# Turning w3 on VectorE in squares of 32 instead of on TensorE

## The chip, the cores and the metric

The kernel runs on one core of a Trainium2 chip. The metric is the device time of one execution in microseconds (us). The core has a matrix engine (TensorE, PE in the profile; its weight loads are shown apart as PEld), VectorE (DVE), ScalarE (ACT), GpSimd (POOL) and SyncE (SP), which here issues the DMAs. Each engine works through its own instructions in order; a semaphore joins them where one needs the result of another. TensorE writes to PSUM, which has eight banks; the other data lie in SBUF, 128 partitions wide.

## What is computed

An mLSTM cell runs over 4 batches, 8 heads, 768 time steps and head size 40. Its output, 3072 tokens of 320 numbers, goes through a multiplicative feed-forward network. The inputs are float64 in memory.

```python
for t in range(S):
    m_new = np.maximum(f_gate[:, :, t] + m, i_gate[:, :, t])
    ...
    C = f_stab[:, :, None, None] * C + i_stab[:, :, None, None] * np.einsum('bhd,bhe->bhde', vt, kt)
    ...
    y[:, :, t] = o * h_tilde / denom
# x: (3072, 320); w1, w2: (320, 1024); w3: (1024, 1024); w_out: (1024, 320)
a = x @ w1
b = x @ w2
h = a * b @ w3
return h @ w_out
```

## The kernel before

**Folding.** The kernel doesn't compute `a * b @ w3` for every token. It folds the two last matrices into one, `w3o = w3 @ w_out` (1024 x 320), and then computes `(a * b) @ w3o`. For the fold, TensorE needs `w3` with its columns on the partitions: for each of eight blocks `ko` of 128 rows of `w3`, a turned tile `w3T[ko]` of 128 partitions by 8 x 128. `w3_mm(ko)` (L240) multiplies its eight squares `w3T[:, ki, :]` with the eight blocks `wo[:, ki, :]` of `w_out`, sums them in the PSUM tile `wp`, and ScalarE brings the sum to `w3o[:, ko, :]`.

**Weights.** They come from memory as pairs of 32-bit words, into one of four `raw` buffers (two parts of the tile `w3o` help out at the start). `fetch` (L179) issues the load of the next of 34 tiles, at most three tiles ahead of the conversions: ten of `w1`/`w2`, eight of `w_out` (128 x 320), sixteen halves of `w3` blocks (128 rows by 512 columns). ScalarE scales the high words (`scale`, L154, the row `raw<-raw`). Then `to_f32` (L158) makes float32 of them with five VectorE instructions (L167 to L171: `ex`, `ex`, `ma`, `ma`, and the target). The fourth one, L170, is the last reader of a `raw` buffer; after it the buffer is free for another load.

**Turning.** A `w3` half that has been converted is put on the list `later`. In the next step `fold` (L216) turns it: `w3_trans` (L228) lets TensorE transpose four squares of 128 x 128 into a PSUM tile `w3p`, and the tile is copied to `w3T`, the first half of a block by VectorE (L238), the second by ScalarE (L236). One step later `fold` runs `w3_mm` of that block.

**Steps.** The main loop has 30 steps `s`; the first 24 run one quarter of work of the cell each (one batch, 128 time steps), the later ones only the network. A step gives TensorE, in this order: `turn(s)`, eight transposes of `k` and `q` (`pt`); `x_trans`, three transposes of the cell's output of two steps before (`px`); `fold` (`wp`, `w3p`); from step 17 on the products with `w3o` (`po`); the products with `w1` and `w2` of two groups (`pa`, `pb`, L499), which step 9 and the steps after it do with 256 columns at a time; their remainders with `wr`; and the cell (`quarter_work`, L292). TensorE's order is fixed by the program. The other engines follow the written order up to step 6 (`pinned`); behind it a scheduler orders them by the readiness that it foresees.

**What waits for what.** `pa` and `pb` are brought together by ScalarE (`a_sb<-pa`, L519) and VectorE (`ab<-pb,a_sb`, L520). All of `pt`, `px`, `wp`, `w3p`, `pa` and `pb` take their turn in four PSUM banks, so the `pt` and `px` of a step use the banks of the `pa` and `pb` of the step before: TensorE waits there until `a_sb` and `ab` of that step are done. In the cell, VectorE multiplies the scores with the weights (`pw<-cell,pw`, L330), which the cell of the next step needs; behind it come the state, `h`, `den` and `y` (L334 to L367), and `y` is turned two steps later.

**SP's queue.** A step's DMAs are issued in the order: two loads `pw<-U_d`, then `k`, `q`, `v`, `o_in`, for two or three steps ahead, then the `raw` loads of that step. SP waits in order for whatever a load's buffer must be free of. Eight semaphores go round for SP's DMAs, so each DMA also waits for the landing of the eighth one before it.

**Which tile when.** By the list `n_cvt`, step 4 and step 5 convert two tiles, steps 6, 7 and 8 three, steps 9 to 15 two. The `w_out` tiles are converted in the steps up to 8, the first `w3` block in step 8, and so on to the last in step 15. So the `w3p` of the first block stand in step 9, its `wp` in step 10, and the last `wp` in step 17.

Of the kernel before, what the change touches and what calls it, by code (L numbers as in the profile page):

```python
# [8 lines left out]
FP = mybir.dt.float32  # L9
# [7 lines left out]
def kernel(  # L17
# [26 lines left out]
    nc = tc.nc  # L44
# [12 lines left out]
    DFF = moe_w1.shape[1]  # L57
    FO = DFF // P
# [7 lines left out]
    wst = ctx.enter_context(tc.tile_pool(name="wst", bufs=2))  # L66
# [15 lines left out]
    def in_order(ins):  # L82

        if last:
            tc.add_manual_dep(ins.ins, last.pop().name, mybir.DependencyInfo(
                mybir.DependencyClass.NoSync, mybir.DependencyReason.DATA), reason="in_order")
        last.append(ins.ins)

    def mm(out, lhsT, rhs, start=True, stop=True):
        in_order(nc.tensor.matmul(out, lhsT=lhsT, rhs=rhs, start=start, stop=stop))  # L90

    def transpose(out, in_, n=P):
        in_order(nc.tensor.transpose(out, in_, ident[0:n, 0:n]))  # L93
# [44 lines left out]
    wo = const.tile([128, FO, DM], FP, name="wo")  # L138
# [4 lines left out]
    CW = 512  # L143
    w1_d, w2_d, w3_d, wo_d = (x.bitcast(U32) for x in (moe_w1, moe_w2, moe_w3, moe_w_out))
# [3 lines left out]
    def raw_tile(n, pieces):  # L148
        raw = idle.pop(0) if idle else wst.tile([128, n, 2], U32, name="raw", tag="raw", bufs=4)
        for r, src in pieces:  # L150
            nc.sync.dma_start(out=raw[r].rearrange("p n two -> p (n two)"), in_=src)
        return raw

    def scale(raw):  # L154
# [3 lines left out]
    def to_f32(dst, raw):  # L158

        n = dst.shape[-1]
        lo, hi = raw[:, :, 0], raw[:, :, 1]
        t = wst.tile([128, n], U32, name="ex", tag="ex", bufs=1)
        r = wst.tile([128, n], U32, name="ma", tag="ma", bufs=1)
        V = nc.vector
        V.tensor_scalar(out=t, in0=hi, scalar1=3, scalar2=None, op0=OP.logical_shift_left)  # L167
        V.scalar_tensor_tensor(out=t, in0=hi, scalar=0x80000000, in1=t, op0=OP.bitwise_and, op1=OP.bitwise_or)  # L168
        V.tensor_scalar(out=r, in0=t, scalar1=0xFF800000, scalar2=None, op0=OP.bitwise_and)
        V.scalar_tensor_tensor(out=r.bitcast(FP), in0=lo, scalar=2.0 ** -52, in1=r.bitcast(FP), op0=OP.mult, op1=OP.mult)  # L170
        V.tensor_tensor(out=dst, in0=t.bitcast(FP), in1=r.bitcast(FP), op=OP.add)  # L171

    def cols(c0, n):
        return slice(2 * c0, 2 * (c0 + n))

    every = slice(0, 128)
    pend, scaled = [], []

    def fetch(kind, i, part):  # L179

        if kind == "w12":
            c0 = part * CW
            if i < 2 * KF:
                wt, src = ((w1, w1_d), (w2, w2_d))[i // KF]
                ko = i % KF
                dst, pieces = wt[:, ko, c0:c0 + CW], [(every, src[ko * 128:(ko + 1) * 128, cols(c0, CW)])]
            else:
                dst, pieces = wr[:, c0:c0 + CW], [(slice(j * REM, (j + 1) * REM), src[KF * P:DM, cols(c0, CW)])
                                                  for j, src in enumerate((w1_d, w2_d))]
        elif kind == "wo":  # L190
            dst, pieces = wo[:, i, :], [(every, wo_d[i * 128:(i + 1) * 128, :])]
        else:
            c0 = part * CW
            dst, pieces = None, [(every, w3_d[i * 128:(i + 1) * 128, cols(c0, CW)])]
        pend.append((dst, raw_tile(dst.shape[-1] if dst is not None else CW, pieces), i, part))

    later = []

    def scale_next():
        scaled.append(pend.pop(0))  # L200
        scale(scaled[-1][1])

    def convert():
        if not scaled:
            scale_next()
        dst, raw, ko, half = scaled.pop(0)
        if dst is None:
            dst = wst.tile([128, CW], FP, name="w3", tag="w3")
            to_f32(dst, raw)
            later.append((dst, ko, half))  # L210
        else:
            to_f32(dst, raw)

    turned_w3 = []

    def fold():  # L216
        while turned_w3:
            w3_mm(turned_w3.pop(0))
        while later:
            w3, ko, half = later.pop(0)  # L220
            w3_trans(w3, ko, half)
            if half:
                turned_w3.append(ko)


    w3T_t = {}

    def w3_trans(w3, ko, half):  # L228
        if half == 0:
            w3T_t[ko] = wst.tile([128, FO, 128], FP, name="w3T", tag="w3T")  # L230
        tp = mps([128, FO // 2, 128], "w3p")
        for j in range(FO // 2):
            transpose(tp[:, j, :], w3[:, j * 128:(j + 1) * 128])
        r = slice(half * (FO // 2), (half + 1) * (FO // 2))
        if half:
            nc.scalar.copy(out=w3T_t[ko][:, r, :], in_=tp)  # L236
        else:
            nc.vector.tensor_copy(out=w3T_t[ko][:, r, :], in_=tp)  # L238

    def w3_mm(ko):  # L240
        w3T = w3T_t.pop(ko)
        wp = mps([128, DM], "wp")
        for ki in range(FO):
            mm(wp, w3T[:, ki, :], wo[:, ki, :], start=(ki == 0), stop=(ki == FO - 1))
        nc.scalar.mul(out=w3o[:, ko, :], in_=wp, mul=UP ** -2)
# [293 lines left out]
    todo = w12[KF * 2 + 1:] + [("wo", i, 0) for i in range(FO)] + [("w3", ko, part) for ko in range(FO) for part in range(2)]  # L539
# [5 lines left out]
    for s in range(len(n_up)):  # L545
# [48 lines left out]
        for _ in range(n_cvt[s] if s < len(n_cvt) else 0):  # L594
            convert()
            converted += 1
# [4 lines left out]
            for ins in keep_order(front):  # L601
                behind.enter_context(tc.issue_after(ins))
    behind.close()
    assert not ups and not downs and not todo and not pend and not later and not turned_w3, (len(ups), len(downs), len(todo), len(pend))
# [1 line left out]
_INS = ['q', 'k', 'v', 'i_gate', 'f_gate', 'o_gate', 'moe_w1', 'moe_w2', 'moe_w3', 'moe_w_out']  # L606
_OUTS = [((3072, 320), 'float32')]
# [25 lines left out]
```

## Time and profile before

| | |
|---|---|
| median of 3 runs | 510.38 us (509.05 to 511.63) |
| the profiled execution | 509.16 us |
| its span on the core | 507.1 us |
| busy: PE, PEld, DVE, ACT, POOL | 472.5, 387.7, 242.7, 161.1, 87.0 us |
| mean granted clock of TensorE | 0.975 |

The span is what the trace covers; some 2 us of the time lie around it. The page's slices cut the span into 40 equal parts, with the busy share of each engine in tenths, and PEclk as the clock that TensorE was granted, in tenths of full speed. A chain of waits goes from the last instruction back to whatever released each one. A row of the timeline reads: start and duration in us, engine, line, operation, out<-in by the program's names, shape, count, and in brackets how long the engine sat idle before it and what ended that. Windows give the busy time of each engine in a stretch. Engine names with a q (SPq) are the queues that issue DMAs.

### The profile page before, as it was taken

The page shows a single profiled execution, that of the slowest core. Times are in us where ns is not written, and L with a number is a line of the kernel's source. Part 1 is how long each engine was busy: PE and PEld are TensorE (multiplying, and loading weights), DVE is VectorE, ACT ScalarE, POOL GpSimd, SP SyncE. Part 2 cuts the span into 40 slices and gives each one's busy share as a digit, 9 for nine tenths or more (in the row PEclk, how much of TensorE's full clock was granted, in tenths as well). Part 3 has the DMA queues.
Part 4 walks back from the last instruction along what each step waited for, and adds up shares of the span by engine and source line. Part 5 has one row for each costly group of instructions (what it writes and reads, how often), then busy time and mean ns, then how long its engine had stood idle before and what let it go on. Part 6 is the DMA issues. An engine that isn't in the chain of part 4 may idle for free.

```text
span 507.1 us, 13454 instructions
## 1 busy us (share of the span) xinstructions
PE 472.5 (93%) x5778; PEld 387.7 (76%) x5778; DVE 242.7 (48%) x504; ACT 161.1 (32%) x421; POOL 87.0 (17%) x163
## 2 busy tenths in 40 slices
PE   3869788896999999999999999999999999899997
PEld 2759677795888788888877777877778778677874
DVE  7787698999877568665440404224032141210110
ACT  4734446355334433523341414222122011111011
POOL 5532223433112111211220202111000000000000
PEclk9979998996999999999999999999999999999999
DMA  8999856599743535421331314131000000000001
GB/s 184 167 207 188 168 104 135 123 220 227 192 115 75 145 107 106 74 49 28 74 63 38 63 38 89 40 74 27 27 14 15 27 13 15 27 0 27 1 14 39
DMA packets 112203, 42.32 MB, mean 83 GB/s; under 512 B 101968, under 2 KB 105232, under 8 KB 112144
## 3 DMA queue, kind: packets, MB, share of 16 engines
q1 hardware_dynamic: 112000, 41.37, 38.5%
q8 instruction: 45, 0.74, 0.7%
q14 instruction: 14, 0.11, 0.1%
q10 hardware_dynamic: 144, 0.10, 0.1%
HBM read 37.42 MB, written 4.03 MB: 82 GB/s over the span
## 4 chain that ended last, share of the span: by engine, by line
PE 77%; DVE 9%; issue 7%; POOL 2%; DMA 2%; ACT 1%; SPq 0%; DVEq 0%; POOLq 0%; ACTq 0%
PE pa L90 21%; PE po L90 20%; PE pb L90 14%; PE cell L90 8%; PE wp L90 7%; PE pt L93 3%; DMA raw<-in_moe_w_dram 2%; DVE h L355 2%; PE w3p L93 1%; PE px L93 1%; PE ub L90 1%; DVE ex L168 1%; DVE ma L170 1%; DVE o_in L365 1%; POOL pw L270 1%
## 5 line engine op out<-in xcount | busy, mean ns | idle before, releaser
L520 DVE TENSOR_TENSOR ab<-pb,a_sb 128x512 f32<-128x512 f32 x48 | 33.2, 691 | 195.6 <-ACT a_sb L519 191.2
L90 PE MATMUL po<-w3o,ab 128*128 128x320 f32 x384 | 105.4, 433 | 1.3 <-DVE h L355 1.3
L90 PEld LDWEIGHTS po<-w3o,ab 128*128 128x128 f32 x384 | 72.2, 190 | 30.7 <-issue 1.5
L90 PE MATMUL pa<-xT,w 128*128 128x256 f32 (+1 forms) x448 | 94.3, 358 | 0.1
L90 PE MATMUL pb<-xT,w 128*128 128x256 f32 (+1 forms) x448 | 92.1, 351 | 0.3 <-issue 0.3
L90 PEld LDWEIGHTS pa<-xT,w 128*128 128x128 f32 x448 | 77.1, 196 | 10.5 <-ACT a_sb L519 0.8
L90 PEld LDWEIGHTS pb<-xT,w 128*128 128x128 f32 x448 | 76.4, 192 | 9.1 <-issue 0.5
L519 ACT ACTIVATE a_sb<-pa 128x512 f32<-128x512 f32 x48 | 28.5, 593 | 117.8 <-PE pb L90 117.8
L289 POOL TENSOR_TENSOR state<-state,decay 128x164 f32<-128x164 f32 x40 | 19.7, 496 | 186.5 <-PE cell L90 132.2
L90 PE MATMUL pb<-xT,wr 64*64 64x256 f32 (+1 forms) x448 | 47.9, 355 | 0.0
L90 PE MATMUL pa<-xT,wr 64*64 64x256 f32 (+1 forms) x448 | 47.9, 355 | 0.0
L270 POOL TENSOR_SCALAR_AFFINE_SELECT pw<-pw 64x512 f32<-64x512 f32 x48 | 34.9, 726 | 54.9 <-ACT pw L268 53.3
L268 ACT ACTIVATE pw<-pw,aT 128x64 f32<-128x64 f32 x160 | 40.5, 336 | 10.9 <-DMA pw<-U_d 9.8
L90 PEld LDWEIGHTS pa<-xT,wr 64*64 64x64 f32 x448 | 28.9, 134 | 14.9 <-issue 6.6
L90 PE MATMUL wp<-wo,w3T 128*128 128x320 f32 x128 | 36.0, 434 | 0.0
L156 ACT ACTIVATE raw<-raw 128x512 f32<-128x512 f32 (+1 forms) x32 | 19.9, 634 | 49.4 <-DMA raw<-in_moe_w_dram 38.1
L527 ACT COPY o_sb<-po 128x320 f32<-128x320 f32 x24 | 10.2, 426 | 74.8 <-PE po L90 74.8
L90 PEld LDWEIGHTS wp<-wo,w3T 128*128 128x128 f32 x128 | 23.7, 190 | 9.2 <-DVE ab L520 0.2
L90 PEld LDWEIGHTS cell<-vbuf,pw 64*64 64x64 f32 x768 | 28.1, 144 | 2.8 <-issue 0.3
L90 PEld LDWEIGHTS pb<-xT,wr 64*64 64x64 f32 x448 | 28.9, 134 | 0.0
L90 PE MATMUL cell<-vbuf,pw 64*64 64x41 f32 x768 | 28.1, 233 | 0.0
L330 DVE TENSOR_TENSOR pw<-cell,pw 128x512 f32<-128x512 f32 x24 | 16.5, 688 | 18.9 <-PE cell L90 15.3
(92 smaller groups left out, 523.0 us busy)
## 6 DMA issues: line engine op xcount, KB each, us to landing
raw<-in_moe_w_dram SPq DMA_DIRECT2D x23, 512.0 KB, 4.5
pw<-U_d SPq DMA_DIRECT2D x40, 128.0 KB, 3.9
kbuf<-in_k_dram SPq DMA_DIRECT2D x24, 160.0 KB, 4.9
qbuf<-in_q_dram SPq DMA_DIRECT2D x24, 160.0 KB, 5.0
vbuf<-in_v_dram SPq DMA_DIRECT2D x24, 160.0 KB, 4.7
o_in<-in_o_gate_dram SPq DMA_DIRECT2D x24, 160.0 KB, 2.9
out_dram<-o_sb SPq DMA_DIRECT2D x24, 160.0 KB, 1.8
raw<-in_moe_w_out_dram SPq DMA_DIRECT2D x8, 320.0 KB, 3.5
```

The source lines that it names most:

```text
L90: in_order(nc.tensor.matmul(out, lhsT=lhsT, rhs=rhs, start=start, stop=stop))
L93: in_order(nc.tensor.transpose(out, in_, ident[0:n, 0:n]))
L156: nc.scalar.mul(out=hi, in_=hi, mul=2.0 ** -111)
L168: V.scalar_tensor_tensor(out=t, in0=hi, scalar=0x80000000, in1=t, op0=OP.bitwise_and, op1=OP.bitwise_or)
L268: nc.scalar.activation(out=pw[:, h, :], in_=src[:, h, :], func=AF.Exp, bias=aT[:, c, b * H + h:b * H + h + 1])
L270: nc.gpsimd.affine_select(out=pw[r], in_=pw[r], compare_op=OP.is_ge, fill=0.0, base=0, pattern=[[0, H], [1, L]], channel_multiplier=-1)
L289: nc.gpsimd.tensor_tensor(out=new, in0=old, op=OP.mult, in1=decay[:, b * NP:(b + 1) * NP, 2 * c + x:2 * c + x + 1] .to_broadcast([P, NP, D1]))
L330: first_read = nc.vector.tensor_tensor(out=pv, in0=ss, in1=pv, op=OP.mult)
L355: nc.vector.tensor_tensor(out=h[r], in0=ph[x], in1=h[r], op=OP.add)
L519: nc.scalar.mul(out=a_sb, in_=pa, mul=UP ** -2)
L520: nc.vector.tensor_tensor(out=ab_t[gr][j][:, fs[0]:fs[-1] + 1, t0:t0 + a_sb.shape[-1]], in0=pb, in1=a_sb, op=OP.mult)
L527: nc.scalar.copy(out=o_sb, in_=po)
```

## The change

`w3` is turned by one VectorE instruction per half, in 32 x 32 squares: a square stays in the 32 partitions in which it lies, and only inside it rows and columns change places. For whole rows to end up on the right partitions, the words are loaded in another order. Partitions 32 j to 32 j + 31 get columns 256 j to 256 j + 255 of `w3`, of 64 rows at a time (two groups of 32). After the turn, partition 32 j + c holds columns 256 j + 32 k + c for k = 0 to 7. The rows of `w_out` are loaded in the same order, so that the sum over `ki` is the same sum in another order. Each of the sixteen `w3` loads and of the eight `w_out` loads becomes four DMAs, one for each 32 partitions; a contiguous run of a `w3` load is 2 KB long, where it was 4 KB.

`w3_trans`, the tile `w3p` and its copies are gone. The turn stands in `convert`, right behind the conversion, a step earlier than before. `fold` keeps a finished block on `ready_w3` for as long as before, so `w3_mm` of a block stands in the same step.

```diff
     def raw_tile(n, pieces):
         raw = idle.pop(0) if idle else wst.tile([128, n, 2], U32, name="raw", tag="raw", bufs=4)
         for r, src in pieces:
-            nc.sync.dma_start(out=raw[r].rearrange("p n two -> p (n two)"), in_=src)
+            dst = raw[r].rearrange("p n two -> p (n two)")
+            if len(src.shape) == 3:
+                dst = dst.rearrange("p (m n) -> p m n", m=2)
+            nc.sync.dma_start(out=dst, in_=src)
         return raw
...
+    CQ = DFF // 4
+    squares = [slice(32 * j, 32 * (j + 1)) for j in range(4)]
...
         elif kind == "wo":
-            dst, pieces = wo[:, i, :], [(every, wo_d[i * 128:(i + 1) * 128, :])]
+            dst, pieces = wo[:, i, :], [(square, wo_d[j * CQ + i * 32:j * CQ + (i + 1) * 32, :])
+                                        for j, square in enumerate(squares)]
         else:
-            c0 = part * CW
-            dst, pieces = None, [(every, w3_d[i * 128:(i + 1) * 128, cols(c0, CW)])]
+            dst, pieces = None, [(square, w3_d[i * 128 + part * 64:i * 128 + (part + 1) * 64, cols(j * CQ, CQ)]
+                                  .rearrange("(m r) n -> r m n", m=2)) for j, square in enumerate(squares)]
...
         dst, raw, ko, half = scaled.pop(0)
-        if dst is None:
-            dst = wst.tile([128, CW], FP, name="w3", tag="w3")
+        if dst is not None:
             to_f32(dst, raw)
-            later.append((dst, ko, half))
-        else:
-            to_f32(dst, raw)
...
+            return
+        w3 = wst.tile([128, CW], FP, name="w3", tag="w3")
+        to_f32(w3, raw)
         if half == 0:
             w3T_t[ko] = wst.tile([128, FO, 128], FP, name="w3T", tag="w3T")
-        tp = mps([128, FO // 2, 128], "w3p")
-        for j in range(FO // 2):
-            transpose(tp[:, j, :], w3[:, j * 128:(j + 1) * 128])
-        r = slice(half * (FO // 2), (half + 1) * (FO // 2))
+        nc.vector.transpose(out=w3T_t[ko].rearrange("c k (m r) -> c m k r", r=32)[:, 2 * half:2 * half + 2],
+                            in_=w3.rearrange("r (m k c) -> r m k c", m=2, k=FO))
         if half:
-            nc.scalar.copy(out=w3T_t[ko][:, r, :], in_=tp)
-        else:
-            nc.vector.tensor_copy(out=w3T_t[ko][:, r, :], in_=tp)
+            turned_w3.append(ko)
+
+    def fold():
+        while ready_w3:
+            w3_mm(ready_w3.pop(0))
+        ready_w3.extend(turned_w3)
+        turned_w3.clear()
```

On TensorE only the `w3p` transposes go; all else keeps its order. On VectorE, ScalarE and SP the scheduler's order behind step 6 changes as well. Lines of the changed kernel are up to six lower or three higher than before.

VectorE, from the `ab` products of step 8 to the cell's work of that step, before: conversions (`ex`, `ma`, `w`) of three `w3` halves stand around `ab` and ahead of the product `pw<-cell,pw`.

```order
L520 TENSOR_TENSOR ab<-pb,a_sb 128x4x128
L167 TENSOR_SCALAR ex<-raw 128x512
L168 SCALAR_TENSOR_TENSOR ex<-raw,ex 128x512
L169 TENSOR_SCALAR ma<-ex 128x512
L520 TENSOR_TENSOR ab<-pb,a_sb 128x4x128
L170 SCALAR_TENSOR_TENSOR ma<-raw,ma 128x512
L171 TENSOR_TENSOR w_1813<-ex,ma 128x512
L167 TENSOR_SCALAR ex<-raw 128x512
L168 SCALAR_TENSOR_TENSOR ex<-raw,ex 128x512
L330 TENSOR_TENSOR pw<-cell,pw 128x2x4x64
```

The same place in the changed kernel, on VectorE again (`pw<-cell,pw` is now L324, `ab` L514):

```order
L514 TENSOR_TENSOR ab<-pb,a_sb 128x4x128 x2
L170 TENSOR_SCALAR ex<-raw 128x320
L171 SCALAR_TENSOR_TENSOR ex<-raw,ex 128x320
L324 TENSOR_TENSOR pw<-cell,pw 128x2x4x64
L328 TENSOR_TENSOR state_1_88<-cell,state_1_88 128x164
L172 TENSOR_SCALAR ma<-ex 128x320
L173 SCALAR_TENSOR_TENSOR ma<-raw,ma 128x320
```

Both `ab` stand together, and at `pw` the conversions have come only to the last tile of `w_out`; the `w3` halves follow later. Between the `pw` of step 7 and that of step 8 stand 23 conversion instructions before and 12 after.

ScalarE, behind the gate of the cell's output (`o_in`), in steps 7 and 8, before:

```order
L251 ACTIVATE o_in<-o_in 128x320
L156 ACTIVATE raw<-raw 128x320 x2
L519 ACTIVATE a_sb<-pa 128x512
L156 ACTIVATE raw<-raw 128x320
L519 ACTIVATE a_sb<-pa 128x512
L268 ACTIVATE pw<-pw,aT 128x64 x8
L279 COPY kT<-pt 128x512
L279 COPY qT<-pt 128x512
L381 COPY xT<-px 128x3x128
```

The same place on ScalarE in the changed kernel:

```order
L245 ACTIVATE o_in<-o_in 128x320
L513 ACTIVATE a_sb<-pa 128x512 x2
L159 ACTIVATE raw<-raw 128x320
L273 COPY kT<-pt 128x512
L273 COPY qT<-pt 128x512
L159 ACTIVATE raw<-raw 128x320
L375 COPY xT<-px 128x3x128
L159 ACTIVATE raw<-raw 128x320
L262 ACTIVATE pw<-pw,aT 128x64 x8
```

Three scalings of `w_out` tiles (`raw`) stood ahead of and between the two `a_sb`; they now stand behind them.

VectorE, at the step border from 9 to 10, in the changed kernel (`w_1845` is the second half of the first `w3` block; the first `wp` of TensorE, in step 10, needs both halves of `w3T`):

```order
L172 TENSOR_SCALAR ma<-ex 128x512
L173 SCALAR_TENSOR_TENSOR ma<-raw,ma 128x512
L174 TENSOR_TENSOR w_1845<-ex,ma 128x512
L324 TENSOR_TENSOR pw<-cell,pw 128x2x4x64
L223 STREAM_TRANSPOSE w3T<-w_1845 128x2x8x32
L328 TENSOR_TENSOR state_1_91<-cell,state_1_91 128x164
```

Before, the same `w3T` was filled behind the `pw` of step 8, a step earlier, here the copy of its first half (`w3T<-w3p`) on VectorE:

```order
L330 TENSOR_TENSOR pw<-cell,pw 128x2x4x64
L334 TENSOR_TENSOR state_1_88<-cell,state_1_88 128x164
L169 TENSOR_SCALAR ma<-ex 128x512
L339 TENSOR_TENSOR state_2_89<-cell,state_2_89 128x164
L351 TENSOR_TENSOR h<-cell,gT 128x2x4x41
L238 COPY w3T<-w3p 128x512
```

So `w3T` of the first block is complete only behind the `pw` of step 9. The second halves of the blocks after it stand ahead of the `pw` of the step before their `wp`, the second block's directly ahead of it.

More of the change, by code (lines that the diff above doesn't have):

```diff
@@ L190, in fetch @@
         elif kind == "wo":
-            dst, pieces = wo[:, i, :], [(every, wo_d[i * 128:(i + 1) * 128, :])]
-        else:
-            c0 = part * CW
-            dst, pieces = None, [(every, w3_d[i * 128:(i + 1) * 128, cols(c0, CW)])]
+            dst, pieces = wo[:, i, :], [(square, wo_d[j * CQ + i * 32:j * CQ + (i + 1) * 32, :])
+                                        for j, square in enumerate(squares)]
+        else:
+            dst, pieces = None, [(square, w3_d[i * 128 + part * 64:i * 128 + (part + 1) * 64, cols(j * CQ, CQ)]
+                                  .rearrange("(m r) n -> r m n", m=2)) for j, square in enumerate(squares)]
         pend.append((dst, raw_tile(dst.shape[-1] if dst is not None else CW, pieces), i, part))
-    later = []
+    w3T_t = {}
+    turned_w3, ready_w3 = [], []
     def scale_next():
@@ L603 @@
     behind.close()
-    assert not ups and not downs and not todo and not pend and not later and not turned_w3, (len(ups), len(downs), len(todo), len(pend))
+    assert not ups and not downs and not todo and not pend and not turned_w3 and not ready_w3, (len(ups), len(downs), len(todo), len(pend))
 _INS = ['q', 'k', 'v', 'i_gate', 'f_gate', 'o_gate', 'moe_w1', 'moe_w2', 'moe_w3', 'moe_w_out']
```

11 lines of the change are left out of this document (removed).

## The prediction

> **What bounds the kernel now.** I read the page's slices first, then the chain of waits in order of time, then windows cut at the step borders (a step begins with TensorE's `pt` transposes), then the timeline of the windows that stand out.
>
> ```profile
> PE   3869788896999999999999999999999999899997
> PEclk9979998996999999999999999999999999999999
> 96.20:113.60 17.40, 14.99 (x273) 13.77 (x267) 16.36 (x40) 9.20 (x27) 3.44 (x7) 0.90 1.03 206
> 113.60:136.00 22.40, 17.97 (x214) 14.57 (x212) 20.33 (x39) 10.59 (x24) 6.67 (x10) 0.77 0.87 210
> 136.00:153.65 17.65, 17.65 (x230) 14.65 (x228) 11.67 (x24) 7.27 (x19) 3.54 (x7) 1.00 0.52 128
> 172.83:190.72 17.89, 17.89 (x228) 14.88 (x229) 12.81 (x26) 7.41 (x19) 3.65 (x6) 1.00 0.46 109
> ```
>
> The columns of a window are its length and the busy time of PE, PEld, DVE, ACT and POOL, then the clock. From 136 us on TensorE is busy all the time. The two windows before it, steps 8 and 9, are different: DVE is busy 16.36 of 17.40 and 20.33 of 22.40 us, TensorE is not, and its granted clock is 0.90 and 0.77. So the change meets two regimes: late steps where each TensorE instruction counts, and two early ones where VectorE's queue decides.
>
> **Late steps.** The chain shows step 10 and the head of step 11:
>
> ```profile
> 137.39 4.31 PE wp L90 x16
> 141.70 0.87 PE w3p L93 x8
> 142.57 1.73 PE pa L90 x8
> 153.68 1.02 PE pt L93 x8
> 155.03 4.46 PE wp L90 x16
> L93 PE MATMUL w3p<-ident,w x64: 272/273/475, 119.5 to 248.6; 128*128 128x128 f32 x64
> ```
>
> Eight `w3p` transposes hold the chain for 0.87 us, not eight times their 273 ns, since they overlap. All 64 go. Step 9 has eight, steps 10 to 16 have eight each: 7 x 0.87 = 6.1 us of pure TensorE time from step 10 on. From `pa` to the next `pt` is 153.68 - 142.57 = 11.1 us, from `pt` to `wp` 155.03 - 153.68 = 1.35 us: a full-speed step without `wp` and `w3p` lasts 12.45 us. Step 9 has no `wp`, yet lasts 22.40. Its 9.95 us too many are the larger prize.
>
> **Where steps 8 and 9 wait.**
>
> ```profile
> 99.22 0.66 PE L93 MATMUL pt<-ident,qbuf 128*128 128x128 f32 x4 [1.88 <-DVE ab L520]
> 100.94 2.92 PEld L90 LDWEIGHTS pa<-xT,w 128*128 128x128 f32 x16 [0.50 <-DVE ab L520]
> 117.36 1.12 PE L93 MATMUL pt<-ident,qbuf 128*128 128x128 f32 x4 [2.65 <-DVE ab L520]
> 96.20:99.20 3.00, 0.77 (x10) 1.00 0.60 192
> 101.00:103.30 2.30, 2.30 (x11) 0.53 1.49 165
> 103.30:104.30 1.00, 1.00 (x11) 1.00 1.05 286
> 117.00:118.00 1.00, 0.64 (x3) 0.50 0.84 274
> 127.00:128.00 1.00, 1.00 (x6) 0.96 0.23 37
> 95.64 0.51 ACT L156 ACTIVATE raw<-raw 128x320 f32<-128x320 f32 x1 [5.06 <-DMA raw<-in_moe_w_out_dram]
> 96.06 0.58 ACT L519 ACTIVATE a_sb<-pa 128x512 f32<-128x512 f32 x1
> 98.91 0.50 ACT L156 ACTIVATE raw<-raw 128x320 f32<-128x320 f32 x1 [2.27 <-DMA raw<-in_moe_w_out_dram]
> 99.30 0.58 ACT L519 ACTIVATE a_sb<-pa 128x512 f32<-128x512 f32 x1
> 98.47 0.69 DVE L520 TENSOR_TENSOR ab<-pb,a_sb 128x512 f32<-128x512 f32 x1
> 103.83 0.68 DVE L330 TENSOR_TENSOR pw<-cell,pw 128x512 f32<-128x512 f32 x1
> 110.33 0.48 DVE L367 TENSOR_TENSOR y<-h,o_in 128x320 f32<-128x320 f32 x1
> 116.62 0.69 DVE L520 TENSOR_TENSOR ab<-pb,a_sb 128x512 f32<-128x512 f32 x1
> 121.91 0.68 DVE L330 TENSOR_TENSOR pw<-cell,pw 128x512 f32<-128x512 f32 x1
> ```
>
> TensorE's `pt`, `px` and `pa` reuse the four PSUM banks of the `pa`/`pb` before them, so they wait for `a_sb` and `ab`. ScalarE held `a_sb` back behind `raw`, whose load had not landed; VectorE held `ab` back behind conversions, to 98.47 and 116.62. After both pauses (3.00 - 0.77 = 2.2 us in 96.2 to 99.2, and 2.65 us before 117.36) the granted clock is near 0.50, the first time to 103.3, the second to about 127.
>
> **The change part by part.** Between the `pw` products at 103.83 and 121.91 stand 23 conversion instructions now, 12 after it; the other conversions move to later steps, where VectorE is busy 12.81 of 17.89 us at most. `a_sb` moves ahead of the loads. I replay steps 8 to 10 by hand, each engine in its new order, with these prices:
>
> ```profile
> L238 DVE COPY w3T<-w3p 128x512 f32<-128x512 f32 x8 | 5.5, 691 | 5.0 <-PE w3p L93 5.0
> L170 DVE SCALAR_TENSOR_TENSOR ma<-raw,ma x32: 480/692/1016, 10.5 to 233.8; 128x512 f32<-128x512 uint32 x24, 128x320 f32<-128x320 uint32 x8
> 96.09 0.41 DVE L167 TENSOR_SCALAR ex<-raw 128x320 uint32<-128x320 uint32 x1
> 143.74 0.43 DVE L167 TENSOR_SCALAR ex<-raw 128x512 uint32<-128x512 uint32 x1
> 146.91 0.43 DVE L167 TENSOR_SCALAR ex<-raw 128x512 uint32<-128x512 uint32 x1
> ```
>
> A conversion takes 2.4 us on 320 columns (96.09 to `ab` at 98.47) and 3.2 us on 512 (143.74 to 146.91). No row shows VectorE's transpose. It isn't below nothing; the shortest row on 128x512 is 0.43 us, the longest single one 1.02 us. I take 0.7, that of the copy that it replaces in size and kind.
>
> Step 8: `ab` begins at 98.47 as now, but `a_sb` is ready for both, so they end at 99.76 and `pa` begins near 100.0, not 100.94. Half of that 0.9 is lost while the clock is 0.50, so step 8 ends at 113.2 (now 113.6). VectorE: conversion 5 of `w_out` to 102.15, `pw` there (now 103.83); the cell chain, which took 7.0 us with seven conversion instructions in it, has five, so 6.1, to 108.3; one conversion to 110.7; both `ab` to 112.0. Nobody on TensorE waits for these in step 9.
>
> Step 9: TensorE runs its 12.45 us from 113.2 to 125.65. VectorE: two instructions, then `pw` of step 8 at 113.2 when TensorE's scores are there, cell chain with three conversion instructions (6.2 us) to 119.4, first `w3` half 3.2 to 122.6, its transpose to 123.3, `ab`, two instructions, `ab`, three instructions to 127.6, `pw` of step 9 to 128.3, and only behind it **the second half's transpose, to 129.0**.
>
> Step 10: `wp` could start at 125.65 + 1.35 = 127.0, but needs that transpose: a new wait of 2.0 us. Both pauses above were followed by half the clock, the shorter one for some 4 us (99.2 to 103.3), so I charge 4 us at half speed, 2.0 us. Behind this wait stand all TensorE work of step 10 and ScalarE's `w3o`, behind that the scaling of the next `w3` half; its conversion then still ends some 3 us before the `ab` of step 10, which waits for TensorE in any case.
>
> Sum: `wp` starts 137.35 - 129.0 = 8.35 us earlier; less 2.0 for the clock; plus 6.1 for 7 x 8 transposes: **12.4 us**. Later steps carry on VectorE 12.81 - 0.69 + 2 x 0.7 = 13.5 us, under the 17.65 - 0.87 = 16.8 us that TensorE needs, so its work is hidden there; cover would end at a transpose of 2.3 us. ScalarE loses eight copies, off the path.
>
> **The loads in quarters.**
>
> ```profile
> 106.79 0.68 ACT L156 ACTIVATE raw<-raw 128x512 f32<-128x512 f32 x1 [0.77 <-DVE h L351]
> L151 SPq DMA_DIRECT2D raw<-in_moe_w_dram x25: 327/367/2374, 2.2 to 199.3; - x25
> DMA to landing us min/median/max: 3.0/4.3/7.6
> raw<-in_moe_w_dram SPq DMA_DIRECT2D x2, 256.0 KB, 4.9
> SPq L151 <- DVE ma L170: 31.6, 9, 7.0
> ```
>
> Twenty-four tiles get three more DMAs each: 72 x 0.37 = 27 us of SP's time. SP waits 31.6 us of 54 to 137 for VectorE to free `raw` buffers, so it has room. A tile leaves 3 x 0.37 = 1.1 us later, and each DMA waits for the eighth one before it. Now the sixth and seventh tile of `w_out` are there at 95.64 and 98.91, when ScalarE starts on them; in quarters that is 97 and 100, and the new order scales them at 100.5 and 101.5, before VectorE's turn at 104.5 and 108.3. The first `w3` half is scaled at 106.79 now and not wanted before 115.5. If a quarter takes the longest landing of now, 7.6 us, not the shortest, 3.0, the two tiles are there at 101.6 and 104.6, late for ScalarE but still ahead of VectorE. So I cost this at nothing; with that cover gone, each microsecond late is one in step 8 or 9. The `k`, `q`, `v` and gate loads behind it on SP slip 1 to 4 us, a step ahead of their use.
>
> The profiled execution took 509.16 us (span 507.1), 1.2 below the median of 510.38. 509.16 - 12.4 = 496.8, and 498.0 from the median; **I predict 497.4**.
>
> **Rivals.**
> 1. *Only TensorE's own time goes.* The backlog on VectorE is fed by landings that now come later, and steps 8 and 9 keep their pauses. Then 6.1 us and the eight transposes of step 9 (twice 0.87 at half clock) go: 7.8, so 502. For it: DVE is nearly full in both steps, and work is moved, not removed. Against it: the pauses hang on `ab` and `a_sb`, which have moved up.
> 2. *The new wait does not slow the clock.* Then 2.0 us less: 495. The trace shows half clock after both pauses, so this is less likely. [...]
> 3. *Slower: SP's eight outstanding DMAs become the bound.* A late step would issue 14 DMAs (8 quarters, 2 of `U`, 4 of cell data). If a landing takes t, the step can't be shorter than 14 t / 8: it passes 16.8 us at t = 9.6. At 12 us the eight steps last 21 each, 3.4 x 8 = 27 us slower than now: 536. For it: 256 KB over half the rows took 4.9 us against 4.5 median for 512 KB, so a cut in size bought nothing. Against: the longest landing is 7.6. [...]
> 4. *The transpose is slow.* Two stand before the first `wp`: at 1.02 us it starts 0.64 us later, 498. Above 2.3 us late steps are bound by VectorE; at 2.8 a step lasts 17.7, as now.
>
> **How the numbers follow.** Forecast 0.62, rival 1 0.20, rival 2 0.10, rival 3 0.04, rival 4 beyond its row's bound 0.04. The range takes the forecast with the new wait absent (another 2.0 us below rival 2: 493) and rival 1 with its median basis (503): 492.5 to 503.5. Half a percent, 2.6 us, is about what a measurement here can tell from no change. Faster: all of the first three, less a little for a fault in the replay, 0.91; same 0.04; slower 0.05.
>
> **What would show it.** Step 9 near 12.5 us at clock 1.0 with no wait on `ab`; first `wp` near 129 with a wait on VectorE's transpose; 16.8 us per step from 11 to 16; a transpose row of 0.7 us. I am wrong if `a_sb` again waits behind a landing, if the clock stays at 0.50 through step 9, or if steps 11 to 16 show TensorE idle.

## The result, and the profile after

| | before | after |
|---|---|---|
| median of four runs | 509.72 us (508.4 to 511.63) | 496.0 us (493.9 to 499.38) |
| the profiled execution, its span | 509.16, 507.1 us | 495.68, 494.0 us |
| ratio of after to before, 95% interval | | 0.9734 (0.967 to 0.9799) |

The change gains 13.1 us between the two spans and 13.7 us between the medians; the forecast was 12.4. The page's slices of the changed kernel, TensorE and its clock:

```profile
PE   3869797899899999999999999999999998999997
PEclk9989998989999999999999999999999999999999
```

Before, the tenth slice (114 to 127 us, step 9) stood at 6 in both rows; now it is 9 in both, and the slice behind it holds an 8. The steps tell more. The windows of steps 8 to 12 of the changed kernel (start:end, length, busy PE, PEld, DVE, ACT, POOL, clock, DMA share, GB/s), cut at the first `pt`:

```profile
96.48:113.33 16.85, 14.57 (x274) 14.15 (x268) 15.69 (x37) 6.21 (x17) 3.67 (x7) 0.90 0.87 174
113.33:125.79 12.46, 12.46 (x208) 10.77 (x204) 11.53 (x26) 5.09 (x14) 1.31 (x3) 1.00 0.91 184
125.79:144.78 18.99, 17.01 (x226) 13.85 (x220) 13.70 (x28) 6.67 (x18) 4.08 (x6) 1.00 0.76 141
144.78:162.92 18.14, 16.99 (x225) 13.80 (x220) 14.43 (x30) 6.77 (x20) 4.00 (x7) 1.00 0.77 149
162.92:179.69 16.77, 16.77 (x225) 13.81 (x220) 13.69 (x28) 6.92 (x21) 3.51 (x6) 1.00 0.51 120
```

Cut in the same way, these steps took 17.37, 21.91, 17.65, 17.79 and 17.89 us before. Steps 8 and 9 of the kernel before, for comparison:

```profile
96.69:114.06 17.37, 14.90 (x268) 13.77 (x268) 16.33 (x40) 9.17 (x26) 3.78 (x6) 0.90 1.05 212
114.06:135.97 21.91, 17.91 (x212) 14.53 (x212) 19.87 (x38) 10.18 (x23) 6.17 (x10) 0.77 0.87 208
```

Step 9 gives 9.45 us by itself. Steps 10 and 11 are longer than before, by 1.34 and 0.35 us, although eight transposes are gone from each. Step 12 gives 1.12, steps 13 to 16 give 0.88 each (16.77 us against 17.65). With 0.5 us in step 8 and 0.2 ahead of it, that adds up to the 13.1 us. The pauses of TensorE in that stretch, from the timeline (start, duration, engine, line, operation, out<-in, and in brackets the idle time ahead and what ended it):

```profile
99.41 0.66 PE L93 MATMUL pt<-ident,qbuf 128*128 128x128 f32 x4 [2.27 <-DVE ab L514]
129.19 2.12 PE L90 MATMUL wp<-wo,w3T 128*128 128x320 f32 x7 [1.98 <-DVE w3T L223]
146.37 0.44 PE L93 MATMUL pt<-ident,kbuf 128*128 128x128 f32 x2 [1.15 <-issue]
```

The first one, at the head of step 8, is left over from before. The second is the new wait for the transpose. The third stands in the middle of step 11's `pt`; the trace shows nothing that it waits for. VectorE's timeline of the changed kernel at the same places:

```profile
98.67 1.29 DVE L514 TENSOR_TENSOR ab<-pb,a_sb 128x512 f32<-128x512 f32 x2
102.05 0.68 DVE L324 TENSOR_TENSOR pw<-cell,pw 128x512 f32<-128x512 f32 x1
111.61 1.29 DVE L514 TENSOR_TENSOR ab<-pb,a_sb 128x512 f32<-128x512 f32 x2
122.14 0.71 DVE L223 STREAM_TRANSPOSE w3T<-w 128x512 f32<-128x512 f32 x1
123.36 0.69 DVE L514 TENSOR_TENSOR ab<-pb,a_sb 128x512 f32<-128x512 f32 x1 [0.51 <-ACT a_sb L513]
128.35 0.69 DVE L223 STREAM_TRANSPOSE w3T<-w 128x512 f32<-128x512 f32 x1
```

The group of all transposes on VectorE (min/median/max in ns, first and last start):

```profile
L223 DVE STREAM_TRANSPOSE w3T<-w x16: 695/711/712, 122.1 to 236.8; 128x512 f32<-128x512 f32 x16
```

### The profile page after: what moved, and what is told of

Same layout as the page of the kernel before. It is cut to its first block, busy times and chain, and to the rows that moved or that the text cites. A ratio compares the mean times of both kernels' runs of the same rounds, so it can differ in the third digit from the quotient of the medians.

```text
span 494.0 us, 13423 instructions
## 1 busy us (share of the span) xinstructions
PE 462.7 (94%) x5714; PEld 380.6 (77%) x5714; DVE 247.5 (50%) x512; ACT 153.5 (31%) x413; POOL 88.6 (18%) x163
## 4 chain that ended last, share of the span: by engine, by line
PE 75%; DVE 9%; issue 7%; DMA 3%; SPq 2%; POOL 2%; ACT 1%; DVEq 0%; POOLq 0%; ACTq 0%
PE po L90 21%; PE pa L90 20%; PE pb L90 14%; PE cell L90 7%; PE wp L90 7%; PE pt L93 3%; SPq L154 2%; DVE h L349 1%; DMA raw<-in_moe_w_dram 1%; DMA pw<-U_d 1%; PE px L93 1%; DMA kbuf<-in_k_dram 1%; PE ub L90 1%; DVE h L345 1%; DVE ma L173 1%
## 5 line engine op out<-in xcount | busy, mean ns | idle before, releaser
L514 DVE TENSOR_TENSOR ab<-pb,a_sb 128x512 f32<-128x512 f32 x48 | 33.0, 690 | 182.0 <-ACT a_sb L513 181.9
L90 PE MATMUL pa<-xT,w 128*128 128x256 f32 (+1 forms) x448 | 93.0, 355 | 0.0
L264 POOL TENSOR_SCALAR_AFFINE_SELECT pw<-pw 64x512 f32<-64x512 f32 x48 | 36.9, 769 | 47.1 <-ACT pw L262 44.6
L365 POOL COPY y<-y 128x64 f32<-128x64 f32 x24 | 7.3, 306 | 110.0 <-DVE y L361 109.8
L324 DVE TENSOR_TENSOR pw<-cell,pw 128x512 f32<-128x512 f32 x24 | 16.4, 685 | 19.0 <-PE cell L90 15.4
```

The costliest lines, as they stand in the source:

```text
L264: nc.gpsimd.affine_select(out=pw[r], in_=pw[r], compare_op=OP.is_ge, fill=0.0, base=0, pattern=[[0, H], [1, L]], channel_multiplier=-1)
L324: first_read = nc.vector.tensor_tensor(out=pv, in0=ss, in1=pv, op=OP.mult)
L365: nc.gpsimd.tensor_copy(out=y_t[n][:, DM:DM + REM], in_=y_t[n][:, KF * P:DM])
L514: nc.vector.tensor_tensor(out=ab_t[gr][j][:, fs[0]:fs[-1] + 1, t0:t0 + a_sb.shape[-1]], in0=pb, in1=a_sb, op=OP.mult)
```

## The experiments

Twelve runs, one kernel among them twice. All step lengths below are cut at the first `pt`, in us. The kernel before is measured on the chip of each run (509.48 to 510.97 us), so ratios are compared, not times. The step lengths come from one profiled execution of each.

| run | median | ratio to before (95%) | steps 8, 9, 10, 11, 12 |
|---|---|---|---|
| before | 509.72 | 1 | 17.37, 21.91, 17.65, 17.79, 17.89 |
| after | 496.0 | 0.9734 (0.967 to 0.9799) | 16.85, 12.46, 18.99, 18.14, 16.77 |
| e1: cut loads alone | 514.75 | 1.0112 (1.0084 to 1.0139) | 16.79, 29.40, 17.65, 17.98, 17.65 |
| e2: turn, whole loads | 506.12 | 0.9935 (0.9904 to 0.9965) | 18.90, 16.91, 20.03, 22.43, 16.77 |
| e5: whole loads, written order to step 9 | 504.39 | 0.9902 (0.988 to 0.9923) | 13.14, 13.21, 22.24, 20.77, 22.99 |
| e8: cut loads, written order throughout | 495.6 | 0.9718 (0.9671 to 0.9764) | 13.15, 13.48, 22.11, 17.72, 16.77 |
| e9: whole loads, written order throughout | 495.95 | 0.9708 (0.9667 to 0.9748) | 13.22, 13.22, 21.71, 17.98, 16.77 |
| e13: e8 with unread transposes on TensorE | 500.12 | 0.9804 (0.9781 to 0.9826) | 13.21, 14.62, 21.75, 17.65, 17.64 |
| e3: VectorE's turn four times | 513.22 | 1.0046 (1.0017 to 1.0075) | 16.82, 12.46, 25.65, 17.71, 17.29 |
| e4: first wp last | 491.76 | 0.9663 (0.9616 to 0.971) | 16.83, 12.46, 16.88, 16.71, 16.78 |
| e4 again | 491.92 | 0.9639 (0.9598 to 0.9679) | 16.85, 12.46, 16.88, 16.72, 16.77 |
| e11: e4, written order to step 7 | 493.82 | 0.9666 (0.9639 to 0.9693) | 13.23, 17.47, 16.87, 16.72, 16.77 |
| e10: written order, one conversion late | 503.62 | 0.9865 (0.9827 to 0.9904) | 13.15, 13.22, 17.08, 18.52, 18.51 |
| e12: written order, no step between turn and wp | 573.49 | 1.1223 (1.1188 to 1.1258) | 13.22, 13.23, 22.74, 29.69, 30.71 |

My theory after seeing the result: the gain of steps 8 and 9 needs two things, VectorE's new order and the turn off TensorE. The first two runs took the change apart. They show that the order of steps 7 and 8 that the prediction counts on comes with the **cut loads**, not with VectorE's transpose.

### The cut loads alone (e1)

The kernel before, with this edit:

```diff
-            dst, pieces = wo[:, i, :], [(every, wo_d[i * 128:(i + 1) * 128, :])]
+            dst, pieces = wo[:, i, :], [(q4, wo_d[i * 128 + q4.start:i * 128 + q4.stop, :]) for q4 in squares]
...
-            dst, pieces = None, [(every, w3_d[i * 128:(i + 1) * 128, cols(c0, CW)])]
+            dst, pieces = None, [(q4, w3_d[i * 128 + q4.start:i * 128 + q4.stop, cols(c0, CW)]) for q4 in squares]
```

> The kernel before, each load of w3 and w_out cut into four DMAs of 32 partitions (the same rows and words); TensorE still transposes w3. Theory A (the order of steps 8 and 9 comes from the cut loads, the gain of it needs the early transpose on VectorE as well): both a_sb ahead of the raw scalings and both ab together in step 8, as after; but the w3 halves are now converted only near 120 and 127 us, and TensorE's w3p of step 9 needs the first of them, so the pause moves from pt to w3p and the gain is eaten: 507 to 515, no clear gain. Theory B (the cut does nothing to the order; the gain is the removed TensorE work and the free banks): order and windows as before, 509 to 511. Theory C (the order alone makes the gain of steps 8 and 9): 501 to 503.

Measured: 1.0112, slower by 5.3 us between the medians. Two rows of TensorE's timeline in step 9:

```profile
123.98 1.09 PE L93 MATMUL w3p<-ident,w 128*128 128x128 f32 x4 [8.57 <-DVE w L171]
128.92 1.09 PE L93 MATMUL w3p<-ident,w 128*128 128x128 f32 x4 [3.85 <-DVE w L171]
```

And one of VectorE's, step 7:

```profile
99.32 1.29 DVE L521 TENSOR_TENSOR ab<-pb,a_sb 128x512 f32<-128x512 f32 x2
```

Both `ab` stand together, as in the changed kernel; step 8 takes 16.79 us, as there. But TensorE needs converted `w3` at the head of step 9. In the new order VectorE converts it only later, so TensorE waits 12.4 us in two pauses. The order without the turn is a loss. Theory A holds; B and C fall.

### The turn without the cut loads (e2)

The changed kernel with whole loads:

```diff
-            dst, pieces = wo[:, i, :], [(square, wo_d[j * CQ + i * 32:j * CQ + (i + 1) * 32, :])
-                                        for j, square in enumerate(squares)]
+            dst, pieces = wo[:, i, :], [(every, wo_d[i * 128:(i + 1) * 128, :])]
...
-            dst, pieces = None, [(square, w3_d[i * 128 + part * 64:i * 128 + (part + 1) * 64, cols(j * CQ, CQ)]
-                                  .rearrange("(m r) n -> r m n", m=2)) for j, square in enumerate(squares)]
+            dst, pieces = None, [(every, w3_d[i * 128:(i + 1) * 128, cols(part * CW, CW)])]
```

> The changed kernel with each load of w3 and w_out as one DMA over 128 partitions; leaves out the reordering of words and rows that the turn in squares needs, so w3o holds other values; the instructions and sizes on the engines are the same. Theory A (the order of steps 8 and 9 comes from the cut loads): VectorE and ScalarE go back to the order of before in step 8, the pauses before pt at 99 and 117 and the half clock come back, and only the transposes' 6.1 to 7.8 us are gained: 501 to 504. Theory B (the removal of the transposes makes the whole gain): step 9 near 12.5 us and 495 to 498.

Measured: 0.9935, some 3.3 us of gain, less than either theory gave. TensorE's longest waits at the head of steps 8, 9, 10 and 11:

```profile
101.46 0.66 PE L93 MATMUL pt<-ident,qbuf 128*128 128x128 f32 x4 [2.16 <-DVE ab L512]
119.61 0.66 PE L93 MATMUL pt<-ident,qbuf 128*128 128x128 f32 x4 [1.41 <-DVE ab L512]
136.49 0.66 PE L93 MATMUL pt<-ident,qbuf 128*128 128x128 f32 x4 [1.38 <-DVE ab L512]
157.58 0.69 PE L93 MATMUL pt<-ident,qbuf 128*128 128x128 f32 x2 [2.09 <-DVE ab L512]
```

The old order is back, as A said, but A missed that it would reach further. VectorE's rows between the first `ab` of step 8 (118.86) and the first of step 9 hold four turned halves:

```profile
119.47 0.70 DVE L221 STREAM_TRANSPOSE w3T<-w 128x512 f32<-128x512 f32 x1
...
123.63 0.71 DVE L221 STREAM_TRANSPOSE w3T<-w 128x512 f32<-128x512 f32 x1
...
130.48 0.71 DVE L221 STREAM_TRANSPOSE w3T<-w 128x512 f32<-128x512 f32 x1
...
135.00 0.71 DVE L221 STREAM_TRANSPOSE w3T<-w 128x512 f32<-128x512 f32 x1
135.74 0.69 DVE L512 TENSOR_TENSOR ab<-pb,a_sb 128x512 f32<-128x512 f32 x1
```

In the changed kernel one turned half (122.14) stands ahead of the `ab` of step 9 (123.36). VectorE converts further ahead of its need here, and TensorE waits for `ab` at the head of four steps instead of one.

### The same loads in the written order (e5, e8, e9)

Is it the order, or do quarters that land sooner help by themselves? The scheduler can be held to the written order (`a_sb`, `ab`, `pw`, the cell chain, then the step's conversions) for more steps. First e2 with

```diff
-    pinned = 7
+    pinned = 10
```

> The run above with the order of steps 8 and 9 held as it is written in the program (a_sb, both ab, pw and the cell chain ahead of the step's conversions) instead of the scheduler's own. Theory A (order plus the turn on VectorE make the gain, the cut loads matter only as what sets the order off): 494 to 499, step 9 without a pause before pt. If the cut loads are needed for themselves (they land sooner): 500 to 504, with raw waits in steps 8 and 9.

Measured: 0.9902, 504.4 us, outside what was expected. Steps 8 and 9 are good (13.14, 13.21), but behind step 9 the scheduler is free again, and steps 11 and 12 take 20.77 and 22.99 us. Step 12 has a `pt` wait of 1.99 us for `ab`, as in e2; step 11 has a pause of 0.99 us in its `pt` that waits for nothing shown, and a mean clock of 0.92. So e5 does not settle the question. The next two hold the order throughout, `pinned = 17`, once with cut loads and once with whole ones.

> The changed kernel, cut loads, with VectorE's and ScalarE's order held as written in the program in every step to 16 (a_sb, ab, pw, cell chain, then the step's conversions). Theory A2 (what decides is only where the conversions stand against ab on VectorE; step 8 has no pause before pt, step 10 waits for the three conversions of step 8 as in the whole-load run, later steps 16.8 us): step 8 and 9 near 13.2 us each, a px wait near 3 us in step 10, 493 to 497, and equal within 1.5 us to the whole-load twin of the next run. Rival (the scheduler's own order of the changed kernel is the better one in late steps too): 499 to 505.

> The same order as in the run before in every step, with each load of w3 and w_out as one DMA over 128 partitions (leaves out the reordering of words and rows, so w3o holds other values). Theory A2 (the cut of the loads matters only as what sets the scheduler's order off): within 1.5 us of the cut-load twin. Rival B2 (quarters land sooner or spread the traffic, and that is worth time by itself): 3 us or more slower than the twin, with waits for raw.

Measured: 495.6 and 495.95 us, on one chip, ratios 0.9718 and 0.9708. With the order held, the cut of the loads is worth nothing that these runs can tell; it matters by the order that it sets off. The quarters do land sooner, in 3.5 and 2.8 us (median) in the changed kernel, where the whole tiles before took 4.5 and 3.5, but in this order nothing on the path waits for that:

```profile
raw<-in_moe_w_dram SPq DMA_DIRECT2D x64, 128.0 KB, 3.5
raw<-in_moe_w_out_dram SPq DMA_DIRECT2D x32, 80.0 KB, 2.8
```

e8 also comes to the time of the changed kernel by another road: steps 8 to 11 take 66.46 us in e8 and 66.44 in the changed kernel. The pause at the head of step 8 is gone (13.15 us), and in its place step 10 waits 3.43 us for an `ab` that stands behind three conversions:

```profile
125.31 0.66 PE L93 MATMUL pt<-ident,qbuf 128*128 128x128 f32 x4 [3.43 <-DVE ab L514]
```

In both, VectorE's backlog of conversions is paid in the step in which it meets an `ab`.

### TensorE's transposes put back (e13)

e8 with eight transposes in each of steps 9 to 16, of data that is always there, read by nobody:

```diff
         fold()
+        for _ in range(2 if 9 <= s <= 16 else 0):
+            tp = mps([128, FO // 2, 128], "w3p")
+            for j in range(FO // 2):
+                transpose(tp[:, j, :], ident)
```

> The changed kernel in the written order of every step (VectorE's and ScalarE's order as in that run), with eight transposes of ident put back on TensorE in each of steps 9 to 16, into the same PSUM tiles as before, read by nobody: the removed TensorE work alone, without the wait for w3, the copies and the other order. Theory A (6.1 of the gain is TensorE's own time, 0.87 us in each of 7 steps; step 9's is covered by step 10's wait for ab): steps 11 to 16 17.6 instead of 16.8 us, 5 to 7 us more than that run, ratio to the kernel before 0.982 to 0.987. Rival (transposes that wait for nothing run beside other work and cost next to nothing; what cost time was their wait and copies): within 2 us of that run, ratio 0.970 to 0.976.

Measured: 0.9804 against 0.9718, 0.0086 x 510 = 4.4 us. The windows of steps 11 and 12:

```profile
145.63:163.28 17.65, 17.65 (x234) 14.65 (x228) 13.02 (x25) 6.35 (x19) 3.18 (x6) 1.00 0.56 104
163.28:180.92 17.64, 17.64 (x232) 14.64 (x228) 13.01 (x25) 6.36 (x19) 3.18 (x6) 1.00 0.63 115
```

17.64 against 16.77 us in the late steps: 0.87 each, the price that the prediction took. In steps 9 and 10 some of it is covered: step 9 is 1.14 us longer, but the wait for `ab` in step 10 is 1.24 us shorter than in e8, since `ab` comes when VectorE is done with its conversions:

```profile
126.73 0.66 PE L93 MATMUL pt<-ident,qbuf 128*128 128x128 f32 x4 [2.19 <-DVE ab L514]
```

The eight transposes of step 10 stand behind that wait. So the two steps together are 0.78 us longer, not 1.74. Steps 11 to 16 pay 5.2 us, less a pause of 0.79 us in step 11 of e8 that is absent here. That makes 5.2 in the profiled executions; the 4.4 of the ratios, with intervals of some 2 us on either side, agree with it. The measured 0.9804 lies just below the range of theory A and outside that of its rival.

### VectorE's transpose four times (e3)

`for _ in range(4):` ahead of the transpose in `convert`; the result is the same.

> The changed kernel with each of VectorE's sixteen transposes done four times, 3 x 0.71 = 2.1 us more each. Theory A (two transposes stand on the path before the first wp; late steps have only some 3 us of VectorE's time left over): first wp about 4.2 us later than the 129.2 of the changed kernel, and late steps of 13.5 + 4.3 = 17.8 instead of 16.8 us: 502 to 508. Rival (VectorE has room everywhere, its transposes are free): within 1 us of the changed kernel, 495 to 497.

Measured: 1.0046 against 0.9734, some 16 us more than the changed kernel, and more than expected. The first `wp`:

```profile
132.77 1.94 PE L90 MATMUL wp<-wo,w3T 128*128 128x320 f32 x3 [6.75 <-DVE w3T L224]
```

It waits 6.75 instead of 1.98 us: 4.8 more, of which two transposes that are 2.1 us longer each explain 4.2. The clock falls behind it (step 10 25.65 us, 0.87 in the mean). Step 11, with its pause of 0.72 us, is 17.71 us long. Where the expectation had 17.8, step 13 takes 19.62 and step 14 21.52: TensorE waits for `ab` again, 2.44 us in step 14. The rival falls: the transposes are hidden because they are short.

### The first wp at the end of its step (e4)

```diff
-        fold()
+        if s != 10:
+            fold()
...
+        if s == 10:
+            fold()
```

> The changed kernel, but the sixteen matmuls of the first wp stand at the end of step 10 instead of behind its pt; same work. Theory A (the wait of 2.0 us for the second half's transpose costs TensorE just its own length): the wait is gone and the time is 1.5 to 2.5 us less than the changed kernel's: 493.5 to 494.5. Rival (step 10 waits for something else then, or the wp at the end delays w3o and the ab of the next step): within 0.5 us of the changed kernel, or slower.

> The run with the first wp last once more, on the chip of the two candidates: 0.966 of the kernel before, as measured; its profile as before, step 11 without the pause in its first pt.

Measured: 0.9663 and 0.9639, with e11 (0.9666) the lowest of all ratios; their intervals touch that of the changed kernel, so the step lengths carry the verdict. Two windows, steps 10 and 11:

```profile
126.11:142.99 16.88, 16.88 (x226) 13.87 (x221) 15.22 (x32) 4.66 (x11) 4.80 (x7) 1.00 0.78 153
142.99:159.70 16.71, 16.71 (x220) 13.76 (x218) 13.34 (x26) 8.67 (x26) 3.70 (x5) 1.00 1.01 174
```

Step 10 loses 2.1 us, just the wait, with the clock at 1.00 in both kernels. Step 11 loses 1.4: the pause of 1.15 us in its `pt` is gone as well, which nobody expected. That makes 3.5, and both runs show it.

### Candidates that fell short (e11, e10, e12)

e11 is e4 with `pinned = 8`, to take away the pause at the head of step 8.

> A candidate: the changed kernel with the first wp at the end of step 10 and the written order held through step 7 (one step longer than now), so that both ab of step 7 stand ahead of that step's conversions. Theory A2: no pause before pt at the head of step 8, no half clock there, step 8 near 13.2 instead of 16.85 us; if the scheduler's order of steps 8 and 9 stays as it is, 3 to 4 us less than the run with the first wp last, 487 to 489. Rival (the conversions put behind ab in step 7 meet the ab of step 8 or 9 instead, so the pause moves): 491 to 497.

The pause is gone there (step 8 13.23 us) and stands at the head of step 9, where the conversions that were put behind the `ab` of step 7 meet that of step 8; the rival was right. By its ratio e11 can't be told from e4:

```profile
113.94 0.66 PE L93 MATMUL pt<-ident,qbuf 128*128 128x128 f32 x4 [2.59 <-DVE ab L514]
```

e10 is e8 with `n_cvt` changed to 2 in step 8 and 3 in step 15, a block's `wp` in the step behind its turn, and `fold` at the end of each step from 10 on.

> A candidate: the changed kernel in the written order to step 16, one conversion moved from step 8 to step 15, and each block's wp at the end of its step. Theory A2: steps 8 and 9 near 13 us without a pause, no px wait in step 10, no wait for a transpose, late steps 16.8: 3 to 5 us less than the run with the first wp last, 486.5 to 489. Rival (one conversion less is not enough, VectorE's backlog still meets an ab in steps 10 to 12): 491 to 496.

Steps 8 to 10 have the lowest sum of all runs (13.15, 13.22 and 17.08 us): one conversion less ahead of the `ab` of step 9 was enough. But with every `wp` last, each later step waits for ScalarE, whose copies of `pt` stand behind `w3o`, `pw` and `raw`:

```profile
144.60 1.56 PE L90 MATMUL pb<-xT,w 128*128 128x256 f32 x6 [1.44 <-ACT kT L271]
PE pb L90 <- ACT kT L271: 9.1, 6, 2.0
```

The second line is from the view of waits, 94 to 330 us: us in total, times, longest. Six such waits make 9.1 us, and steps of 18.5 us and more. Neither theory had named it. With `wp` ahead of `pa`, as in e8, these waits are absent; that the four microseconds of `wp` cover the copy there is argued from their place, not tested.

e12 moves the conversion to step 9 and puts `fold` back at the head of steps 11 and on, still one step after the turn.

> A candidate: the written order to step 16, one conversion moved from step 8 to step 9, the first block's wp at the end of step 10 and the others at the head of their step. Theory A2: steps 8 and 9 near 13.2, step 10 16.9 without a px wait, a pause of some 2 us at the head of step 11 behind three conversions (and half the clock for some 4 us if it is as long as that), then 16.8: 489 to 493. Rival (the kT wait of the run with every wp last is there again): 495 or more.

The replay behind this was wrong: at the head of a step the conversions of the step before still stand behind its cell chain. The view of waits:

```profile
PE wp L90 <- DVE w3T L223: 69.3, 6, 11.7
```

Six waits of up to 11.7 us each, and the time is 573 us. This shows what `ready_w3` is worth, which keeps a whole step between the turn and its `wp`.

## Why the prediction was right

**The regime.** That step 9 and not the late steps holds the larger prize is shown: 9.45 of 13.1 us. (The prediction cut step 9 at 113.60 and 136.00 and found 22.40 us and 9.95 too many; between the first `pt` it is 21.91 and 9.46.)

**VectorE's order.** The replay by hand of steps 8 and 9 held to less than a microsecond: `ab` to 99.96 (99.76 in the text), `pw` of step 7 at 102.05 (102.15), step 9 from 113.33 (113.2) and 12.46 us long (12.45) at clock 1.00. What the prediction did not say is that this order comes from the cut loads (e1 has it, e2 does not), and that neither part would have done alone: 1.0112 for the order without the turn, 0.9935 for the turn without the order, 0.9734 for both. e13 narrows down what "the turn off TensorE" has to mean: with sixty-four unread transposes back on TensorE most of the gain stays, so in e1 it was TensorE's wait for `w3` in step 9 that ate it, not its work. Whether a turn that stays on TensorE, but a step later, would keep the gain of steps 8 and 9 was not run.

**VectorE's transpose.** 0.7 was taken from the copy; the row says 0.711. e3 shows that its length matters twice on the path, as the terms had it, and then in the late steps, by more than they had: the sum of 17.8 us a step left out that TensorE waits again for an `ab` behind the conversions.

**TensorE's transposes.** 7 x 0.87 = 6.1 was the term. The price holds (e13), and so does the sum: steps 10 to 16 together are 2.95 us shorter than before, with two pauses of 1.98 and 1.15 us in them that were not there, which makes 6.1. Where step 10 waits for `ab` on VectorE (e8 against e13), the transposes ahead of that wait, those of step 9, are covered by it.

**The new wait.** Foreseen with its cause, its place (129.0; 129.19) and its length (2.0; 1.98). **The clock behind it was the mis-sized term**: 2.0 us were charged for 4 us at half speed, and TensorE kept 1.00 (129.19 to 133.00). That part of rival 2 was right, partly by luck: in e5 a wait of 1.99 us had a mean clock of 0.54 behind it (last section), and nothing in the prediction could tell the two apart. The other three executions of the changed kernel had mean clocks of 0.973 to 0.975, against 0.982 in the profiled one; where they lost it is not on record. e4 confirms the size of the wait: without it, step 10 is 2.1 us shorter.

**What made up for it.** The pause of 1.15 us in step 11 was not foreseen. 12.4 + 2.0 - 1.15 = 13.25, and 13.1 was measured. The forecast was this close partly by luck: the two misses have opposite signs.

**The loads.** Costed at nothing, and e8 against e9 shows nothing: 0.35 us between the medians. That is so for their landing alone; by way of the order they carry the larger share. The rival in which eight outstanding DMAs bound the steps falls: it needed landings of over 9.6 us, and quarters landed in 3.5.

**Rival 1** (the pauses stay) was wrong for this kernel but describes e2, where the pauses stay; even its 502 was too good there (506.12).

## What to carry to other kernels

Before crediting a gain to the operation that was moved, build each part of the change alone and compare the engines' orders: here a cut of the loads that is worth nothing with the order held set off the order on which the larger share of the gain rests, and alone it made the kernel slower. When an engine carries a backlog, reordering moves the pause to the next place where the backlog meets something that others wait for (e8, e11); only less work ahead of that place (e10's steps 8 to 10), or a consumer that is put later (e4), takes it away. A step that is good by itself may have been the cover of another engine's copy (e10), so look at what a moved block was hiding.

The lowest ratio here is that of the changed kernel with the first `wp` at the end of step 10 (e4). Steps 8 to 10 of e10 with the late steps of e4 would save another 2.7 us by their lengths (43.45 against 46.17), an estimate; no run joins the two.

## What the runs showed of the hardware

**Pauses and the clock.** The new wait of the changed kernel lasted 1.98 us, and the clock behind it stayed at 1.00. The wait of e5 ahead of 168.29 lasted 1.99 us, and the clock from there to 172.00 was 0.54 in the mean. So the length alone does not decide. In the traces of the two kernels, before and after, the points at which the granted clock changed lie whole multiples of 3.41 us apart; in the changed kernel, for one, it fell to 0.50 at 100.62 and was back at 1.00 at 104.03. The changed kernel around the new wait, cut whole multiples of 3.41 us behind 104.03 (length, busy PE, clock, DMA share, GB/s):

```profile
124.51:127.92 3.41, 2.70 (x101) 1.00 1.03 204
127.92:131.34 3.42, 2.15 (x8) 1.00 0.82 109
131.34:134.75 3.41, 3.41 (x15) 1.00 0.76 186
```

And e5:

```profile
165.20:168.61 3.41, 1.42 (x41) 1.00 0.50 154
168.61:172.03 3.42, 2.79 (x10) 0.50 0.57 150
```

The pause of the changed kernel, 127.21 to 129.19, is split by these cuts: TensorE is idle for 0.71 us of one stretch and 1.27 of the next. That of e5 lies inside one stretch and leaves it idle for 1.99 of 3.41 us; the stretch behind it runs at 0.50. Between 60 and 480 us of the traces of the two kernels, cut in this way, five stretches at full clock were followed by half clock; they had been idle for 1.86 to 2.55 us. The 236 that were followed by full clock had been idle for 1.45 us at most. Those are the bounds of these two traces alone: step 11 of e5 has a mean clock of 0.92 with 1.62 us of idle TensorE in all. That the two pauses of some 2 us differed by where they fell is my reading of these rows; no run moved a pause to test it. By these rows one stretch at half clock costs up to 1.7 us, half of 3.41 (an estimate); the prediction charged 2.0 and took it as certain.

**A pause tied to a place in the program.** The changed kernel, e3, e5, e8 and e9 pause 0.72 to 1.15 us between the second and third `pt` of step 11, with nothing shown that it waits for. They have the same TensorE instructions up to there. So has e2, where all of step 11 holds only 0.13 us of idle TensorE beside its wait of 2.09 us for `ab`. e4, e10, e11 and e12 (another order of the `wp`) and e13 (sixteen transposes more) don't have the pause. DMA traffic is not a likely cause: in e9 the DMA share around the pause was 0.14.

```profile
144.56 0.44 PE L93 MATMUL pt<-ident,kbuf 128*128 128x128 f32 x2 [0.99 <-issue]
```

```profile
143.00:146.40 3.40, 2.41 (x28) 1.88 (x18) 2.44 (x6) 3.27 (x8) 1.91 (x4) 1.00 0.14 48
```

What it is stays open.
